# Two steps of a top-k attention kernel change engines: places behind the scores filled on GpSimd, two of nine penalties on VectorE

## The chip, the cores and the metric

The kernel runs on one core of a Trainium2 chip. A core has five engines with queues of their own: TensorE (PE in the profile; its weight loads are PEld), VectorE (DVE), ScalarE (ACT), GpSimd (POOL) and SyncE (SP, which here issues most transfers). Each works its queue in order, and they meet at semaphores. The metric is the device time of one execution in microseconds, taken as the median of several runs.

## The reference, cut to what matters

Attention over 8 batches and 8 heads (sequence 576, head size 64), where each query keeps only its 32 best keys, followed by a mixture of 8 experts over the 4608 tokens:

```python
scores = scale * np.matmul(q, k.transpose(0, 1, 3, 2))
kth = np.partition(scores, -top_k, axis=-1)[..., -top_k:-top_k + 1]
mask = scores >= kth                       # top_k = 32
scores = np.where(mask, scores, -1000000000.0)
...                                        # softmax over the kept ones
return np.matmul(attn, v).astype(np.float32)
# then, per token: skip by the sign of x @ w_skip, choose the expert by argmax of x @ w_gate,
# y = gate * relu(x @ w1[e]) @ w2[e], out = x + y
```

## The kernel before, in words

The 64 heads are worked as 32 pairs. For a pair, the scores of 2 x 576 queries are made in 9 row tiles (`NR = 9`) of 128 queries by `S = 576` keys. Each row tile s goes through a chain that finds its 32nd largest score:

- `qk` (line 666, TensorE): the products, into one of three PSUM buffers r.
- `chunk` (675, VectorE): the 8 largest of each of 7 pieces of the row, seven MAX8 into cand; `cand` (681, 683): five steps, MAX8 and MATCH_REPLACE in turn, that take the 24 largest out of these 56 into cl.
- `take` (694, ScalarE): the scores copied from PSUM to xc. `above_out` (689, ScalarE): r = sign of the 24th candidate less the score, with the sum over the row in CN, which tells how many scores lie above.
- `push_out` (697, GpSimd): xw = xc times r, so that scores above the 24th turn negative. `fill` (706, VectorE): the places behind the 576 scores in xw get large numbers or zero, as many large ones as CN says, so that the next step always finds the 32nd score at place 8. `window` (713, VectorE): the 8 largest of xw, into wn; wn's last is the 32nd score.
- `below_out` (710, ScalarE): PEN = relu(32nd - score), 0 for the keys that are kept.

Two pairs later at most, `block` (804, TensorE) makes the scores again with keys on the partitions, and adds PEN times nbi = -BIG on the identity, so that dropped keys vanish in the exponential (825, ScalarE, into PT). `values` multiplies by v and sums on TensorE in a mode of 32 columns; `prep` makes the next pairs' queries and keys, split into HI (576) and LO = TT - HI (579) on GpSimd; `add` (851, GpSimd) sums two PT tiles; `maxes` (767) and `flags` (717 to 719) are small copies on GpSimd. In the stretch from some 470 to 630 us GpSimd and VectorE also work on `route`, the choice of experts for the first half of the batches.

The order of all this is not written by hand. Every step is a `Task` with an engine, a duration, a due time and the tasks that it waits for; `Plan.run` picks, engine by engine, the task that can start first, and among these the one due first. Due times are the row's number plus an entry of the table `K` plus one of `FINE` for the row's place i in its pair. The result is a fixed program. `DRAIN` is what the plan charges for a change of TensorE's mode.

The lines that the change is about, before:

```python
nc.vector.tensor_scalar(xw()[:, S:S + NF].rearrange("p (a c) -> p a c", a=3), wo[:, :, 0:3], CN[:, s:s + 1], BIG, op0=OP.is_ge, op1=OP.mult)
...
nc.scalar.activation(pen, XC[s], AF.Relu, bias=least, scale=-1.0)
```

After the attention, from about 838 us on, the experts' products fill TensorE (lines 1138 to 1163); `checks` looks at CN and FL there, for rows on which the short way to the 32nd score does not hold.

Of the kernel before, what the change touches and what calls it, by code (L numbers as in the profile page):

```python
# [32 lines left out]
K = dict(qk=-8.256, cand=-59.344, kt=-7.645, push=-28.261, count=0.262, window=9.704, kth=1.605, rf=117.784, pen=-29.958, u0=9.017, u1=9.316, av=-2.884, a0=2.011, a1=2.549, a2=-15.308, co=32.529, sm=-64.563, ca=53.074, tx=-30.308, rt=20.468, rd=-1.415, rs=1.694, pp=14.93, ps=4.136, mx=35.641, f3=20.33, f4=9.022, f5=-15.635, ex=-32.099, us=-0.03, cs=-26.207, ch=-11.218, ce=-46.256, lg=-25.29, ld=12.434, hl=-17.564, hs=-33.172, moe=-7.644)  # L33

FINE = dict(qk=(-10.57, -22.223, -7.096, -21.366, 2.278, -119.12, -31.346, -10.762, 4.455), ch=(12.505, 76.162, -10.027, -38.815, -20.633, 31.276, 34.186, -28.766, -4.283), cand=(6.613, -24.489, -6.913, -22.336, 35.534, -77.941, -24.764, 58.647, -21.15), tx=(-96.011, 71.695, -8.092, -28.201, -15.853, -10.927, -86.098, -6.646, -69.204), kt=(-9.574, -35.926, 21.492, -20.724, -58.083, 108.198, 75.445, 16.722, -3.221), push=(-37.539, 9.983, 6.119, 6.494, -84.073, 20.264, 2.344, 2.351, 10.939), fill=(-25.14, 8.838, 43.271, 3.475, -104.037, -36.948, 24.579, -38.407, 8.32), window=(11.533, -43.047, -0.139, 16.434, -11.305, -22.448, 36.514, 47.528, 5.356), rf=(-13.011, 128.284, 95.339, -40.779, -41.656, -3.528, -16.581, -1.309, -7.056), u=(-2.26, -2.822, -2.506, -3.277, 1.006, -2.132, 3.038, -0.939, -1.738), ex=(-29.429, 18.435, -78.347, -71.269, 37.149, -83.914, -14.847, -34.82, -52.676), f1=(1.311, -59.185, -32.839, -20.531, 4.006, 77.409, -35.268, 14.784, -2.373, -92.948, 24.393, -155.546, -98.645, -15.536, -44.446), f2=(-1.024, -53.705, 3.596, -4.574, -2.423, -3.931, -69.348, -59.52, -5.109), f3=(12.258, -23.157, 17.272, -15.562, 18.297, 1.275), f4=(-10.133, 2.408, -52.184), f5=(0.895, -4.039, -13.889, -126.479, -18.842, -21.09, 31.156, 23.265, -33.592), pp=(5.828, 32.569, 33.595), pa=(-22.396, 0.136, 19.457), hl=(-35.088, -24.202, -29.517, 32.477), mx=(-2.834, 4.967, -17.41, -30.151, -39.559, -52.101), sm=(6.246, -8.842, 17.735, -15.926, -5.444, 7.721))


@with_exitstack
def tile_kernel(ctx, tc, q, k, v, w_skip, w_gate, w1, w2, out):
# [140 lines left out]
    class Plan:  # L180
# [65 lines left out]
        def run(self):  # L246
            picks, dirty = {}, set(ENGS)
            while self.n:
                for e in dirty:
# [24 lines left out]
                for h in x.give:
                    h.give(x)
                    dirty.add("PE")
                for y in x.users + x.next:
                    y.left -= 1
                    y.ready = max(y.ready, x.done + wait(e, y.eng) if y in x.users else t + x.dur)
                    if not y.left:  # L280
                        self.todo[y.eng].append(y)
# [365 lines left out]
    def row(s):  # L647
# [37 lines left out]
        def above_out():  # L685


            RR[s] = wk.tile([P, S], BF, name="r", bufs=3)
            nc.scalar.activation(RR[s], XC[s], AF.Sign, bias=CL[p][:, i, 23:24], scale=-ODD, accum_out=CN[:, s:s + 1])  # L689
# [9 lines left out]
        def xw():  # L699
            if s not in XW:  # L700
                XW[s] = wk.tile([P, S + NF], F32, name="xw", bufs=2)
            return XW[s]

        def fill():

            nc.vector.tensor_scalar(xw()[:, S:S + NF].rearrange("p (a c) -> p a c", a=3), wo[:, :, 0:3], CN[:, s:s + 1], BIG, op0=OP.is_ge, op1=OP.mult)

        def below_out():
            pen, least = PEN[p][:, PS * i + REM:PS * (i + 1)], WN[p][:, i, 7:8]
            nc.scalar.activation(pen, XC[s], AF.Relu, bias=least, scale=-1.0)  # L710

# [547 lines left out]
    def checks():  # L1259
# [7 lines left out]
        for u in range(NR):  # L1267
# [17 lines left out]
        nc.vector.scalar_tensor_tensor(okr, lasf, 1.0, okr, op0=OP.not_equal, op1=OP.mult)  # L1285
        nc.vector.tensor_scalar(okr, okr, 2.0 ** -30, None, op0=OP.is_ge)
        yield
# [267 lines left out]
```

## Time and profile before

| | us |
|---|---|
| median of 3 runs | 1139.01 (1138.16 to 1139.36) |
| profiled execution | 1137.82 |
| its span in the profile | 1135.8 |

Granted TensorE clock over the span: 0.988 of full speed. Busy shares of the whole span, and busy tenths in 40 equal slices of 28.4 us:

```profile
PE 1088.7 (96%) x13000; PEld 934.5 (82%) x13000; DVE 974.7 (86%) x5226; ACT 920.3 (81%) x1902; POOL 752.9 (66%) x949
DVE  8999999999999999999999999999965656655541
ACT  5899999999999999999999999999783533444430
POOL 7678788887787888888998788888784121222211
```

The first 29 or 30 slices are the attention part, the rest the experts. Busy time of PE is modelled at the ends of matmuls, so a busy PE is not PE at its peak. In rows of groups, "busy, mean ns of one" is followed by the idle time just before and what ended it; in rows of waits stand the total, the number and the longest.

### The profile page before, as it was taken

Reading aid. Unit: us, or ns where it says so; the run is one execution under the profiler, and the core shown is the slowest. Engines: PE = TensorE matmul, PEld = TensorE weight load, DVE = VectorE, ACT = ScalarE, POOL = GpSimd, SP = SyncE. Lnnn points to the kernel's source line nnn. Section 1 sums busy time; section 2 is a strip of 40 time slices with the busy share of each in tenths; the row PEclk is TensorE's granted clock in tenths of the full one; section 3 lists DMA queues with packets and bytes.
Section 4 is the critical chain, followed back from the end, with each engine's and each line's share of the span. In section 5 each row is a group of like instructions: output and inputs, shape, how many; then the busy total and the mean of one; then the engine's idle time right before and its main releaser. Section 6 shows DMA issues by size and latency. Waiting matters only on the chain. (4 is left out here: it accounts for less than half of the span.)

```text
span 1135.8 us, 37472 instructions
## 1 busy us (share of the span) xinstructions
PE 1088.7 (96%) x13000; PEld 934.5 (82%) x13000; DVE 974.7 (86%) x5226; ACT 920.3 (81%) x1902; POOL 752.9 (66%) x949
## 2 busy tenths in 40 slices
PE   7999999999999999999999999999899999999996
PEld 5788888888888888888788888888678888999995
DVE  8999999999999999999999999999965656655541
ACT  5899999999999999999999999999783533444430
POOL 7678788887787888888998788888784121222211
PEclk8899999999999999999999999999999999999998
DMA  7645555656555566665545555665147654554300
GB/s 166 126 96 120 125 127 130 148 131 142 117 132 123 125 137 136 148 134 120 127 106 128 127 125 130 138 153 114 44 123 240 187 191 161 169 170 164 121 20 27
DMA packets 239256, 149.06 MB, mean 131 GB/s; under 512 B 141657, under 2 KB 204633, under 8 KB 239057
## 3 DMA queue, kind: packets, MB, share of 16 engines
q1 hardware_dynamic: 232192, 136.19, 49.8%
q0 software_dynamic: 3840, 9.47, 2.4%
q8 instruction: 105, 1.72, 0.6%
q10 hardware_dynamic: 3024, 0.90, 0.3%
q14 instruction: 95, 0.77, 0.2%
HBM read 76.57 MB, written 25.31 MB: 90 GB/s over the span
## 5 line engine op out<-in xcount | busy, mean ns | idle before, releaser
L697 POOL TENSOR_TENSOR xw<-xc,r 128x576 f32<-128x576 f32 x288 | 370.1, 1286 | 117.6 <-ACT r L689 115.4
L675 DVE MAX8 cand<-r 128x8 f32<-128x82 f32 (+1 forms) x2016 | 368.8, 233 | 1.0 <-ACT PEN L710 0.7
L689 ACT ACTIVATE r<-xc,cl 128x576 bf16<-128x576 f32 x288 | 226.4, 786 | 11.7 <-DVE cl L681 8.2
L710 ACT ACTIVATE PEN<-xc,wn 128x576 bf16<-128x576 f32 x288 | 223.3, 787 | 3.6 <-DVE wn L713 3.3
L713 DVE MAX8 wn<-xw 128x8 f32<-128x585 f32 x288 | 217.2, 755 | 2.2 <-POOL xw L697 2.0
L804 PE MATMUL r<-QH,KK 128*128 128x256 f32 (+1 forms) x640 | 187.4, 320 | 6.8 <-ACT PT L825 5.5
L694 ACT ACTIVATE xc<-r 128x576 f32<-128x576 f32 x288 | 186.5, 657 | 6.2 <-DVE cl L681 2.2
L804 PE MATMUL r<-QL,KK 66*128 66x256 f32 (+1 forms) x640 | 172.9, 298 | 0.0
L825 ACT ACTIVATE PT<-r 128x576 f32<-128x576 f32 x256 | 167.7, 656 | 3.1 <-PE r L804 3.1
L681 DVE MAX8 cl<-cand 128x8 f32<-128x28 f32 (+2 forms) x864 | 165.7, 193 | 4.1
L666 PE MATMUL r<-KK,QH 128*128 128x288 f32 x640 | 158.3, 337 | 6.5 <-DVE KK L622 2.4
L1067 POOL DMA_INDIRECT out_dram<-ot,idx x24 | 24.4, 1016 | 190.4 <-DVE ot L1066 146.9
L804 PE MATMUL r<-nbi,PEN 128*128 128x128 bf16 (+1 forms) x1632 | 125.9, 215 | 15.1 <-ACT PT L825 11.1
L666 PE MATMUL r<-KK,QL 65*128 65x288 f32 x640 | 134.0, 300 | 0.0
L804 PEld LDWEIGHTS r<-QH,KK 128*128 128x128 f32 x640 | 117.8, 190 | 15.9 <-ACT PT L825 11.2
L1030 ACT ACTIVATE hi<-raw 128x1024 fp32r<-128x1024 f32 x64 | 67.0, 1056 | 78.7 <-PE py L1163 70.7
L1033 DVE TENSOR_TENSOR lo<-raw,hi 128x1024 fp32r<-128x1024 f32 x60 | 73.2, 1224 | 62.1 <-ACT hi L1030 62.1
L666 PEld LDWEIGHTS r<-KK,QH 128*128 128x128 f32 x640 | 98.2, 193 | 26.5 <-issue 12.8
L804 PEld LDWEIGHTS r<-QL,KK 66*128 66x128 f32 x640 | 118.7, 191 | 0.0
L804 PEld LDWEIGHTS <-PEN 128*128 128x128 bf16 x1632 | 87.3, 98 | 33.5 <-issue 14.2
L666 PEld LDWEIGHTS r<-KK,QL 65*128 65x128 f32 x640 | 103.1, 193 | 0.2 <-DVE QL L622 0.2
L683 DVE MATCH_REPLACE8 cand<-cl,cand 128x28 f32<-128x28 f32 (+1 forms) x576 | 103.0, 179 | 0.0
(272 smaller groups left out, 2453.2 us busy)
## 6 DMA issues: line engine op xcount, KB each, us to landing
raw<-in_moe_w_dram SPq DMA_DIRECT2D x64, 512.0 KB, 4.0
KK<-HI SPq DMA_DIRECT2D x62, 288.0 KB, 3.5
QH<-HI SPq DMA_DIRECT2D x124, 144.0 KB, 3.5
KK<-LO SPq DMA_DIRECT2D x62, 144.0 KB, 3.2
QL<-LO SPq DMA_DIRECT2D x62, 144.0 KB, 3.3
raw<-in_k_dram SPq DMA_DIRECT2D x64, 128.0 KB, 3.0
V<-in_v_dram SPq DMA_DIRECT2D x32, 256.0 KB, 3.3
out_dram<-xd SPq DMA_DIRECT2D x28, 288.0 KB, 3.3
```

The lines of the kernel that those rows point to most:

```text
L666: nc.tensor.matmul(R(u, w), t[0:k0, c:c + P], KH[i2][0:k0, HB * hd + u:HB * hd + w], start=(k0 == P and x == 0), stop=(k0 < P and x == len ...
L675: nc.vector.max(C[s][:, c], R(CH[c], CH[c + 1]))
L681: nc.vector.max(L[:, 4 * r:4 * r + 8], c)
L683: nc.vector.match_replace(c, L[:, 4 * r - 4:4 * r + 4], c, LOWEST)
L689: nc.scalar.activation(RR[s], XC[s], AF.Sign, bias=CL[p][:, i, 23:24], scale=-ODD, accum_out=CN[:, s:s + 1])
L694: nc.scalar.activation(XC[s], R(), AF.Copy)
L697: nc.gpsimd.tensor_tensor(xw()[:, 0:S], XC[s], RR[s], op=OP.mult)
L710: nc.scalar.activation(pen, XC[s], AF.Relu, bias=least, scale=-1.0)
L713: nc.vector.max(WN[p][:, i], XW[s])
L804: nc.tensor.matmul(*ops, start=half not in [x[0] for x in todo[:j]], stop=half not in rest, skip_group_check=turned)
L825: return pl.add("ACT", 0.535, due + K["ex"] + FINE["ex"][at], lambda: nc.scalar.activation(dst, st["r"], AF.Exp, scale=scale), x, give=[h])
L1033: eng.tensor_tensor(WLO[w][i], WRAW[w][i], WHI[w][i], op=OP.subtract)
```

## The change

1. `fill` moves from VectorE to GpSimd: a subtraction of two tiles, wo - CN, into 7 places instead of 9. For this the scores in xc are scaled by SMALL = 2^-30 (in the same copy), so that any positive whole number is larger than every score and any negative one smaller.
2. For row tiles i = 3 and 7 of each pair, `below_out` moves from ScalarE to VectorE, as a comparison with one tensor as source: 1 where the score is below the 32nd, else 0. BIG becomes 2^120, which restores the weight of the scaled differences of the other seven.
3. The planner's costs: changes of TensorE's mode (INTO, DRAIN), a gap ahead of some products (GAP), rows 0.535 and units 0.785 for each; the two moved steps with their new durations; two added conditions (a pair's transposes behind the HI cast of the pair before, row products of i > 2 behind the units of two pairs before); all of K and FINE are new numbers.

```diff
-BIG = 2.0 ** 90
+BIG = 2.0 ** 120
+SMALL = 2.0 ** -30
+BELOW = (3, 7)
...
-DRAIN, TURN = 0.2, 43.29
+DRAIN, INTO, GAP, TURN = 0.02, 0.13, 0.083, 43.29
...
-    NF = 9
+    NF = 7
...
-    wo = cp.tile([P, 3, 4], F32, name="wo")
-    nc.gpsimd.iota(wo, pattern=[[-6, 3], [-2, 4]], base=S - 2 * (TOPK - 7), ...)
-    nc.gpsimd.memset(wo[:, 2, 1:4], -2.0 * S)
+    wo = cp.tile([P, NF], F32, name="wo")
+    nc.gpsimd.iota(wo, pattern=[[-2, NF]], base=S - 2 * (TOPK - 7) + 1, ...)
...
                     if x.mode != self.mode:
-                        t += DRAIN
+                        t += INTO if x.mode == 32 else DRAIN
                         self.mode = x.mode
+                    if x.kind and not self.round:
+                        t += GAP
...
-            nc.scalar.activation(RR[s], XC[s], AF.Sign, bias=CL[p][:, i, 23:24], scale=-ODD, accum_out=CN[:, s:s + 1])
+            nc.scalar.activation(RR[s], XC[s], AF.Sign, bias=CL[p][:, i, 23:24], scale=-ODD / SMALL, accum_out=CN[:, s:s + 1])
...
-            nc.scalar.activation(XC[s], R(), AF.Copy)
+            nc.scalar.activation(XC[s], R(), AF.Copy, scale=SMALL)
...
-            nc.vector.tensor_scalar(xw()[:, S:S + NF].rearrange("p (a c) -> p a c", a=3), wo[:, :, 0:3], CN[:, s:s + 1], BIG, op0=OP.is_ge, op1=OP.mult)
+            nc.gpsimd.tensor_tensor(xw()[:, S:S + NF], wo, CN[:, s:s + 1].to_broadcast([P, NF]), op=OP.subtract)
...
-            nc.scalar.activation(pen, XC[s], AF.Relu, bias=least, scale=-1.0)
+            if i in BELOW:
+                nc.vector.tensor_scalar(pen, XC[s], least, None, op0=OP.is_lt)
+            else:
+                nc.scalar.activation(pen, XC[s], AF.Relu, bias=least, scale=-1.0)
...
-        fx = A("DVE", 0.129, s + D_["push"] + J("fill"), fill, rr, OUTW[-2:-1])
+        fx = A("POOL", 0.2, s + D_["push"] + J("fill"), fill, rr, OUTW[-2:-1])
...
-        kx = PENNED[s] = A("ACT", 0.672, s + D_["rf"] + J("rf"), below_out, wx, TU.get(p - 2))
+        kx = PENNED[s] = A(*(("DVE", 0.42) if i in BELOW else ("ACT", 0.672)), s + D_["rf"] + J("rf"), below_out, wx, TU.get(p - 2))
```

What this makes of the order is seen in pair 8, one of the even pairs, whose order repeats in the pairs before and after. Names in the rows: out<-in, with buffer numbers; lines of the changed kernel lie 4 to 7 further down (chunk 679, cand 685 and 687, window 720, the penalty on VectorE 715, push 701, fill 710, LO 583, HI 580, sum 858).

VectorE around row 3 of the pair and its window, before (the fill of row 3 is `xw_4648`, its window five chunks later):

```order
L683 MATCH_REPLACE cand_4615<-cl_4342,cand_4615 128x7x4
L706 TENSOR_SCALAR xw_4648<-wo_123,CN_126 128x9
L681 MAX cl_4342<-cand_4615 128x8
L675 MAX cand_4663<-r2_156 128x8
L683 MATCH_REPLACE cand_4615<-cl_4342,cand_4615 128x7x6
L675 MAX cand_4663<-r2_156 128x8
L681 MAX cl_4342<-cand_4615 128x8
L675 MAX cand_4663<-r2_156 128x8 x5
L713 MAX wn_4343<-xw_4648 128x8
```

The fill is gone from there. VectorE now, from row 3's penalty (`PEN0_201<-xc_4614`) to row 4's window (`xw_4714`):

```order
L679 MAX cand_4709<-r2_155 128x8
L687 MATCH_REPLACE cand_4665<-cl_4359,cand_4665 128x7x6
L679 MAX cand_4709<-r2_155 128x8
L685 MAX cl_4359<-cand_4665 128x8
L679 MAX cand_4709<-r2_155 128x8 x3
L715 TENSOR_SCALAR PEN0_201<-xc_4614,wn_4360 128x576
L685 MAX cl_4359<-cand_4709 128x8
L720 MAX wn_4360<-xw_4714 128x8
```

The penalty stands between a row's last chunk and its first candidate step, two places ahead of the next window. Further on in the pair, VectorE at row 7, its window (`xw_4912`) and its penalty (`xc_4832`):

```order
L685 MAX cl_4899<-cand_4898 128x8
L720 MAX wn_4360<-xw_4912 128x8
L679 MAX cand_4928<-r0_153 128x8 x2
L715 TENSOR_SCALAR PEN0_201<-xc_4832,wn_4360 128x576
L685 MAX cl_4899<-cand_4928 128x8
L679 MAX cand_4998<-r2_155 128x8
```

Here the penalty follows its own row's window at two chunks' distance. GpSimd at the end of the pair before, from row 7's push (`xw_4877`) to the next pair's first row (`xw_5014`):

```order
L697 TENSOR_TENSOR xw_4877<-xc_4800,r_4852 128x576
L943 TENSOR_TENSOR lg_158<-lg_158,lgt_4875 128x2x2x9
L576 CAST HI_129<-TT_128 128x640 x2
L697 TENSOR_TENSOR xw_4942<-xc_4872,r_4903 128x576
L579 TENSOR_TENSOR LO_130<-TT_128,HI_129 128x640
L697 TENSOR_TENSOR xw_5014<-xc_4967,r_4995 128x576
```

And now, from the sum ahead of it to the next pair's first row (`xw_5012`):

```order
L858 TENSOR_TENSOR sum_4847<-PT0_130 128x576
L950 TENSOR_TENSOR lg_157<-lg_157,lgt_4835 128x2x2x9
L580 CAST HI_128<-TT_127 128x640 x2
L774 CAST NM0_207<-cl_4359 128x4
L710 TENSOR_TENSOR xw_4912<-wo_123,CN_125 128x7
L701 TENSOR_TENSOR xw_4912<-xc_4832,r_4876 128x576
L583 TENSOR_TENSOR LO_129<-TT_127,HI_128 128x640
L710 TENSOR_TENSOR xw_4979<-wo_123,CN_125 128x7
L701 TENSOR_TENSOR xw_4979<-xc_4885,r_4926 128x576
L710 TENSOR_TENSOR xw_5012<-wo_123,CN_125 128x7
```

Each fill now stands ahead of its push, and a LO subtraction directly behind row 7's push, where the two HI casts stood between that push and the next one.

More of the change, by code (lines that the diff above doesn't have):

```diff
@@ new lines @@
+DRAIN, INTO, GAP, TURN = 0.02, 0.13, 0.083, 43.29
+K = dict(qk=-8.543, cand=-15.083, kt=0.641, push=-15.471, count=0.262, window=-4.445, kth=1.605, rf=24.177, pen=-29.958, u0=7.338, u1=11.714, av=-8.454, a0=-11.233, a1=-5.352, a2=13.3, co=39.882, sm=-23.106, ca=53.074, tx=12.855, rt=7.719, rd=13.521, rs=0.505, pp=-1.174, ps=14.228, mx=-2.994, f3=12.416, f4=52.975, f5=21.746, ex=-16.886, us=-3.268, cs=-21.736, ch=-3.905, ce=-12.018, lg=15.965, ld=12.313, hl=4.176, hs=-7.114, moe=7.778)
+FINE = dict(qk=(-12.87, -13.071, -0.344, -26.066, 4.762, -15.372, -7.663, -0.205, 5.146), ch=(3.582, 14.88, -6.257, -19.664, 1.084, 4.045, 6.598, -14.85, 8.09), cand=(-6.274, 0.043, -19.338, 9.135, 3.386, 4.725, -6.454, -13.932, -19.095), tx=(-2.799, 16.941, 5.973, -1.758, -14.865, 25.1, -5.775, -4.793, -16.542), kt=(5.187, -8.053, -11.18, 9.905, 13.525, -13.317, -12.528, 9.006, 4.973), push=(11.95, 8.137, 4.28, 2.957, -7.633, -17.997, 6.536, 14.0, -1.622), fill=(-2.25, -25.583, -7.589, -4.801, -9.466, 2.719, 0.196, 13.815, -9.43), window=(7.295, -3.217, 17.228, 8.542, -15.004, -7.732, 21.554, 14.087, -0.102), rf=(-19.604, 13.641, -0.544, -17.392, -7.293, 11.12, -8.241, 9.439, -2.146), u=(5.016, 3.153, 6.815, 9.245, 0.177, 3.228, 8.968, 10.542, -3.11), ex=(-4.089, -9.336, -14.813, 8.475, -12.628, 3.76, -7.448, 20.175, 2.359), f1=(17.187, -2.992, 1.004, 5.716, -0.479, 52.969, -11.568, 21.046, -4.222, 6.826, -4.425, -13.086, -13.917, 1.599, -2.937), f2=(19.781, -9.808, 3.596, 18.59, -8.525, -3.931, -8.164, -16.856, -5.109), f3=(14.766, 11.443, -3.211, -11.216, -13.714, -15.862), f4=(7.784, 9.035, -35.608), f5=(-8.395, -16.083, -14.55, 15.552, -3.473, 13.474, -8.661, 14.986, 19.967), pp=(-11.882, 9.279, -25.414), pa=(-16.671, -6.231, 19.662), hl=(-4.523, -0.717, 3.198, 15.585), mx=(-28.121, 4.967, -17.41, -14.055, -39.559, -52.101), sm=(10.394, -8.842, 17.735, -13.775, -5.444, 7.721))
@@ L567, in prep @@
             due = NR * p - K["pp"] + K["ps"] * j
-            x = pl.add("PE", 0.11 * len(g), due + FINE["pp"][j], turn(h, g), [LOADED[nm, p] for nm in nms], take=h)
+            x = pl.add("PE", 0.11 * len(g), due + FINE["pp"][j], turn(h, g), [LOADED[nm, p] for nm in nms],
+                       [HIGH[nm, p - 1] for nm in nms if p > 1], take=h)
             y = pl.add("ACT", 0.478 if len(g) > 1 else 0.265, due + 0.1 + FINE["pa"][j], lambda h=h, nms=nms: put(h, nms), x,
@@ L590, in prep @@
             due = NR * p - K["hl"] + K["hs"] * nm
-            x = pl.add("POOL", 0.73, due + FINE["hl"][2 * nm], lambda nm=nm: high(nm), puts[nm], CFREE.get(nm))
+            x = HIGH[nm, p] = pl.add("POOL", 0.73, due + FINE["hl"][2 * nm], lambda nm=nm: high(nm), puts[nm], CFREE.get(nm))
             y = SPLIT[nm, p] = pl.add("POOL", 1.53, due + FINE["hl"][2 * nm + 1], lambda nm=nm: low(nm), x)
@@ L602, in prep @@
             COPIED[p] += c
-    CFREE = {}
+    CFREE, HIGH = {}, {}
     def first(puts):
@@ L722, in row @@
         J = lambda nm: FINE[nm][i]
-        x = ROWQ[s] = A("PE", 0.54 * len(st), s + D_["qk"] + J("qk"), qk, ready(p, i >= NM), CHUNK.get(s - 1), take=h, lag=0.09, kind="row")
+        x = ROWQ[s] = A("PE", 0.535 * len(st), s + D_["qk"] + J("qk"), qk, ready(p, i >= NM), CHUNK.get(s - 1), TU.get(p - 2) if i > 2 else None, take=h, lag=0.09, kind="row")
         chs = []
@@ L822, in f @@
             st["r"] = block(p, whats, h.t, pl.turned)
-        x = pl.add("PE", 0.86 if len(whats) == 1 else 1.65, due + FINE["u"][at], f, after, war, MAXED[p, 0], ready(p, whats[-1][0]), None if p else KOCOPIED, take=h, kind="unit")
+        x = pl.add("PE", 0.785 * len(whats), due + FINE["u"][at], f, after, war, MAXED[p, 0], ready(p, whats[-1][0]), None if p else KOCOPIED, take=h, kind="unit")
         TU[p].append(x)
@@ L1273, in checks @@
             yield
-        nc.vector.scalar_tensor_tensor(okr, FL[:, 0], 2.0 ** 30, FL[:, 1], op0=OP.mult, op1=OP.add)
+        nc.vector.scalar_tensor_tensor(okr, FL[:, 0], 2.0 ** 30 * SMALL, FL[:, 1], op0=OP.mult, op1=OP.add)
         nc.vector.scalar_tensor_tensor(okr, okr, 0.0, FL[:, 3], op0=OP.is_ge, op1=OP.mult)
@@ L1285, in checks @@
         nc.vector.scalar_tensor_tensor(okr, lasf, 1.0, okr, op0=OP.not_equal, op1=OP.mult)
-        nc.vector.tensor_scalar(okr, okr, 2.0 ** -30, None, op0=OP.is_ge)
+        nc.vector.tensor_scalar(okr, okr, 2.0 ** -30 * SMALL, None, op0=OP.is_ge)
         yield
```

4 lines of the change are left out of this document (1 added, 3 removed).

## The prediction

> **What bounds the kernel now.** I read the busy time by stage first, then the waits inside the longest even stage, then single instructions there. The stages: the attention part does 32 pairs of heads with 9 row tiles each; 119.68 to 447.64 us is its even middle, 472.46 to 631.27 us the part where routing work is mixed in, 631.27 to 782.30 us even again.
>
> ```profile
> core 0: us, PE busy (x) PEld busy (x) DVE busy (x) ACT busy (x) POOL busy (x), PEclk, DMA share, GB/s
> 119.68:447.64 327.96, 321.38 (x4603) 275.30 (x4604) 324.37 (x1990) 326.21 (x703) 262.06 (x313) 1.00 0.58 132
> 472.46:631.27 158.81, 152.69 (x2182) 128.99 (x2171) 155.96 (x940) 153.75 (x327) 139.62 (x185) 1.00 0.58 126
> 631.27:782.30 151.03, 147.99 (x2120) 126.98 (x2124) 149.43 (x917) 150.22 (x325) 121.26 (x149) 1.00 0.59 132
> ```
>
> The same stretches counted for the push on GpSimd alone (line 697, one for each row tile):
>
> ```profile
> 119.68:447.64 327.96, 150.62 (x117) 1.00 0.58 132
> 472.46:631.27 158.81, 69.42 (x54) 1.00 0.58 126
> ```
>
> 117 rows are 13 pairs, so a pair takes 327.96 / 13 = 25.23 us; 54 rows are 6 pairs of 26.47 us. VectorE and ScalarE are busy for 99% of the even stretch, and asked for their waits there the profile lists none for either. The other two wait:
>
> ```profile
> PE r L804 <- ACT PT L825: 6.6, 26, 0.3
> POOL xw L697 <- ACT r L689: 51.2, 65, 2.0
> ```
>
> So two engines are the bound together: taking work from one alone gains nothing. TensorE has 327.96 - 321.38 = 6.58 us without work, 0.51 us a pair, and becomes the bound once both give that up. GpSimd has 65.9 us, 5.07 us a pair, 51.2 of it waiting for the signs r.
>
> **What each part costs, for a pair of 25.23 us.** An instruction's price is the time from its start to the next one's, since neighbours overlap. ScalarE first, then VectorE:
>
> ```profile
> 409.14 0.78 ACT L710 ACTIVATE PEN<-xc,wn 128x576 bf16<-128x576 f32 x1
> 409.81 0.78 ACT L689 ACTIVATE r<-xc,cl 128x576 bf16<-128x576 f32 x1
> ```
> ```profile
> 408.82 0.21 DVE L706 TENSOR_SCALAR xw<-wo,CN 128x9 f32<-128x9 f32 x1
> 408.94 0.09 DVE L683 MATCH_VALUE_LOAD cand<-cl,cand 128x8 f32 x1
> ...
> 409.12 0.24 DVE L675 MAX8 cand<-r 128x8 f32<-128x82 f32 x1
> 409.28 0.20 DVE L681 MAX8 cl<-cand 128x8 f32<-128x56 f32 x1
> 409.40 0.68 DVE L675 MAX8 cand<-r 128x8 f32<-128x82 f32 x4
> 410.11 0.19 DVE L681 MAX8 cl<-cand 128x8 f32<-128x28 f32 x1
> 410.22 0.75 DVE L713 MAX8 wn<-xw 128x8 f32<-128x585 f32 x1
> 410.89 0.07 DVE L683 MATCH_VALUE_LOAD cand<-cl,cand 128x8 f32 x1
> ```
>
> *ScalarE.* Two of nine penalties leave: 2 x 0.67 (409.14 to 409.81) = 1.34 us. It stands at 23.9 us and is no longer the bound. The factor on the copy to xc adds no instruction, and the setup loses one memset: 0.
>
> *VectorE, the fills leave.* 9 x 0.12 (408.82 to 408.94) = 1.08 us.
>
> *VectorE, the two penalties come.* No such instruction is in the trace before. The nearest have one tensor source:
>
> ```profile
> L706 DVE TENSOR_SCALAR xw<-wo,CN x288: 193/211/228, 19.1 to 838.9; 128x9 f32<-128x9 f32 x144
> L499 DVE TENSOR_SCALAR rlo<-i,rank x3: 280/280/281, 874.2 to 874.6; 128x128 bf16<-128x128 f32 x3
> L1286 DVE TENSOR_SCALAR okr<-okr x1: 311/311/311, 978.0 to 978.0; 128x288 f32<-128x288 f32 x1
> ```
>
> Line 499 has the form of the new one: a scalar for each partition, f32 in, bf16 out. From 9 to 128 columns the form grows by 280 - 211 = 69 ns, 0.58 ns a column, which makes 211 + 567 x 0.58 = 540 ns of 576 columns. The fill lasts 211 ns and holds the engine for 120, so the penalty holds it for 540 - 91 = 0.45 us. The upper end is the window's MAX8, one column at a time, 0.67 us (410.22 to 410.89); the lower is line 1286 twice, for twice its columns, less one start (the fill's 211 ns) and the overlap: 2 x 311 - 211 - 91 = 0.32 us. I take 0.45, from the row with the same form: + 0.90 us.
>
> *VectorE, the new order.* A step that reads the one just in front of it starts late: the first candidate step after its own row's last chunk starts 0.26 us after that chunk (four chunks from 409.40, 0.15 apart, so 409.85 to 410.11), behind a chunk of another row 0.16 us (409.12 to 409.28). The order has three such places a pair before and one after: - 2 x 0.10 = - 0.20 us. The window loses 2 of 585 columns, 9 x 2 x 750 / 585 ns (the 0.75 us of 410.22) = - 0.02 us. Together: 25.23 - 1.08 + 0.90 - 0.20 - 0.02 = 24.83 us, if nothing new waits.
>
> *The new wait.* [...]
>
> ```profile
> L461 DVE CAST rri<-rmx x3: 172/681/866, 505.1 to 871.2; 128x20 int32<-128x20 f32 x1, 128x15 int32<-128x15 f32 x1, 128x5 int32<-128x5 f32 x1
> L462 DVE TENSOR_SCALAR rri<-rri x3: 158/161/1044, 510.1 to 871.6; 128x20 int32<-128x20 int32 x1, 128x15 int32<-128x15 int32 x1, 128x5 int32<-128x5 int32 x1
> L473 DVE TENSOR_SCALAR base<-base x1: 2216/2216/2216, 802.7 to 802.7; 128x8 f32<-128x8 f32 x1
> ```
> ```profile
> 791.21 0.68 DVE L461 CAST rri<-rmx 128x15 int32<-128x15 f32 x1
> 792.10 1.04 DVE L462 TENSOR_SCALAR rri<-rri 128x15 int32<-128x15 int32 x1
> ```
> ```profile
> 790.42 1.44 POOL L851 TENSOR_TENSOR sum<-PT 128x576 f32<-128x576 f32 x1
> 791.81 1.30 POOL L697 TENSOR_TENSOR xw<-xc,r 128x576 f32<-128x576 f32 x1
> ```
>
> The cast of 0.17 us ends at 791.89, 0.03 us behind the sum (790.42 + 1.44 = 791.86); the next one, 0.16 us alone, ends at 793.14, 0.03 behind the push (793.11). [...] A penalty that comes while a push runs can therefore wait 0 to 1.3 us, and the whole VectorE queue behind it (candidates, windows, and through them ScalarE's penalties and TensorE's units).
>
> [...]
>
> Which of 0 to 1.3 us it is, the order decides. Row 3's penalty stands two places ahead of row 4's window, which needs the end of row 4's push anyway, so what it waits behind that push is mostly the window's own wait: I take 0. Row 7's stands a window and two chunks, 0.67 + 2 x 0.15 = 0.97 us, behind its own push's end at the earliest; GpSimd goes from that push to the LO subtraction, the first of these rows:
>
> ```profile
> L579 POOL TENSOR_TENSOR LO<-TT,HI 128x640 fp32r<-128x640 f32 x62 | 96.8, 1563 | 0.5
> L697 POOL TENSOR_TENSOR xw<-xc,r 128x576 f32<-128x576 f32 x288 | 370.1, 1286 | 117.6 <-ACT r L689 115.4 <-DVE cand L675 0.4 <-DVE wn L713 0.2
> L943 POOL TENSOR_TENSOR lg<-lg,lgt 64x9 f32<-64x9 f32 x62 | 12.5, 201 | 0.5
> ```
>
> At most 1.56 - 0.97 = 0.59 us of LO are left then, and none if the window came 0.6 us after the push; past that the next push can be in the way. I take 0.2, nearer to none. VectorE then stands at 24.83 + 0.2 = 25.03 us. Both ends stay for the range: 0, and 1.3 us each.
>
> *GpSimd, the fills come.* One between 64x9 and the 128x5 cast lasts about 0.2 us (the row of line 943, 201 ns): 9 x 0.2 = 1.8 us of the 5.07 us that are free, and two penalties can keep it out for 0.45 us each: 2.7 us, 22.9 of 25. On the path each fill stands ahead of its push (row 5's behind), so the window of a row may come 0.2 us later; the lower end is 0, since the 51.2 us of waiting over 117 rows (0.44 a row) show that GpSimd is ahead, the upper 1.8 us a pair if every window waited for its push. No window does now, and the order keeps a row or more between: 0.
>
> *TensorE* loses nothing but gets the two added conditions on the plan (the raw tiles' transposes behind the HI cast, row products behind older units). They move instructions and add none; the order keeps them. If they cost, its 0.51 us of idle time is the cover and is then gone.
>
> *The sum.* 25.23 - 25.03 = 0.20 us a pair over the 13 + 6 even pairs and some 3 of the first 119.68 us: 22 x 0.20 = 4.4 us. The routing stretch: GpSimd is busy 139.62 of 158.81 us; 54 fills add 10.8 and 12 penalties up to 5.4, 155.8 us, so nothing is left to gain there, and 0 to 4 us to lose if its work bunches; I take 0. Everything behind 838 us is unchanged and only starts sooner. The profiled execution took 1137.82 us, 2.0 more than its span of 1135.8; the median of the runs is 1139.01, 1.2 above it. So 1133.4 us for a profiled run, and 1139.0 - 4.4 = 1134.6 us for the median: 1135.
>
> **Rivals.**
>
> *The lock eats more than was freed (slower).* The place is the same two penalties, the price is GpSimd's remaining instruction. Met at random, GpSimd busy 22.9 of 25 us and its instructions 1.3 to 1.6 us long, a penalty waits about 0.9 x 0.65 = 0.6 us, and the rows of lines 461, 462 and 473 show 0.7, 0.9 and 2.0. From 0.4 us a pair on, 24.83 + 0.4, VectorE is back at 25.23. At 0.35 each, 25.53 us, it is 22 x 0.3 = 6.6 us slower, and the routing stretch, where GpSimd is full, adds 2: 1148 us. At 0.6 each, 1159. For it: the order of the two engines is fixed and repeats every pair, so an unlucky place is met every time. Against: GpSimd hangs on VectorE through the signs, so it is not random, and part of a wait is the next window's own. Chance 0.32. [...]
>
> *Nothing moves.* [...] Chance 0.18.
>
> *TensorE becomes the bound.* Both penalties come between two GpSimd instructions or behind one that ends, the waits vanish, and the pair falls until TensorE is full, 24.72 us by its recorded idle time: 22 x 0.51 = 11.2 us, with 1 to 3 us more at the start and in the routing part: 1126. For it: ScalarE's 1.34 us of room let the signs come earlier and keep GpSimd ahead. Chance 0.2, within faster.
>
> **How the numbers follow.** My forecast, a small gain of 3 to 8 us, has 0.30, TensorE's bound 0.20: faster by over 0.2% (2.3 us, about what a measurement of this kernel can tell from none) 0.50, within it 0.18, slower 0.32. The range leaves out 2 in 10: the lower end is TensorE's bound with 3 us more from routing, 1123; the upper the first rival between its two prices, 1151. The forecast's own range is 1131 to 1137.
>
> **What the profile after would show.** Right: line 715 on VectorE at about 0.54 us, ScalarE with 7 penalties a pair and idle 3 to 5% of the even part, VectorE still at 99% without waits, GpSimd near 88%, pairs of about 25.0 us. The lock: line 715 far over 0.54 us, its end just behind a GpSimd instruction's end. [...] TensorE the bound: its idle time gone and waits of VectorE for its row products. Wrong altogether: windows that wait for pushes, the fills' 0.2 us on the path after all; or route work stretched well past 158.81 us.

## The result, and the profile after

The changed kernel takes 1154.87 us (median of 6 runs, 1145.38 to 1160.09); the kernel before took 1139.18 in the runs beside it. The ratio is 1.013, 95% interval 1.0104 to 1.0156: slower by 15.7 us, where a gain of 4 was forecast. The profiled execution took 1154.68 us with a span of 1152.8, 17.0 more than the span before.

The penalty on VectorE, all 64 of them (shortest, median and longest, in ns):

```profile
L715 DVE TENSOR_SCALAR PEN<-xc,wn x64: 497/952/3904, 35.3 to 857.1; 128x576 bf16<-128x576 f32 x64
```

Two populations make this row. Row 3's penalty takes 497 to 510 ns in all pairs from 1 to 16; row 7's takes about 1430 in most of them. Pair 8, whose order the prediction spoke of, on VectorE and then on GpSimd (start, duration):

```profile
250.11 0.75 DVE L720 MAX8 wn<-xw 128x8 f32<-128x583 f32 x1
250.78 0.38 DVE L679 MAX8 cand<-r 128x8 f32<-128x82 f32 x2
251.07 1.43 DVE L715 TENSOR_SCALAR PEN<-xc,wn 128x576 bf16<-128x576 f32 x1
252.42 0.18 DVE L685 MAX8 cl<-cand 128x8 f32<-128x28 f32 x1
```
```profile
249.19 1.56 POOL L583 TENSOR_TENSOR LO<-TT,HI 128x640 fp32r<-128x640 f32 x1
250.71 0.19 POOL L710 TENSOR_TENSOR xw<-wo,CN 128x7 f32<-128x7 f32 x1
250.87 1.28 POOL L701 TENSOR_TENSOR xw<-xc,r 128x576 f32<-128x576 f32 x1
252.12 0.45 POOL L710 TENSOR_TENSOR xw<-wo,CN 128x7 f32<-128x7 f32 x1
```

The penalty comes 0.20 us after row 8's push has started, and ends 0.35 us after the push does, as if the push had to end first: 1.43 - 0.50 = 0.93 us of wait. The small fill behind, 0.20 us elsewhere, takes 0.45 and ends 0.07 us behind the penalty, as if now the penalty were ahead of it. This is what the prediction calls the lock: a VectorE instruction that ends behind one of GpSimd's as if it had to wait for it, as the steps of lines 461 and 462 did in the kernel before (0.03 us behind). But it is not behind the LO subtraction: it is behind the push.

By stage. The rows are the stretch of pairs 2 to 16, of pairs 17 to 24 (with routing work), and, inside the first, of pair 11 alone:

```profile
core 0: us, PE busy (x) PEld busy (x) DVE busy (x) ACT busy (x) POOL busy (x), PEclk, DMA share, GB/s
72.00:459.00 387.00, 377.16 (x5322) 316.78 (x5316) 380.73 (x2191) 362.00 (x781) 325.59 (x496) 0.99 0.56 129
459.00:674.30 215.30, 207.91 (x2901) 172.24 (x2893) 209.69 (x1188) 195.11 (x419) 195.99 (x308) 0.99 0.55 124
302.60:333.00 30.40, 27.13 (x353) 22.97 (x353) 27.80 (x147) 24.31 (x53) 21.07 (x34) 0.89 0.48 109
```

An undisturbed pair takes 25.4 us (25.2 before). Pair 11 takes 30.4, and its granted clock is 0.89. What happened at its start, where row 7 of the pair before is still in work, on GpSimd, VectorE and TensorE:

```profile
301.69 1.28 POOL L701 TENSOR_TENSOR xw<-xc,r 128x576 f32<-128x576 f32 x1
302.93 0.20 POOL L710 TENSOR_TENSOR xw<-wo,CN 128x7 f32<-128x7 f32 x1
303.09 1.27 POOL L701 TENSOR_TENSOR xw<-xc,r 128x576 f32<-128x576 f32 x1
304.33 1.53 POOL L583 TENSOR_TENSOR LO<-TT,HI 128x640 fp32r<-128x640 f32 x1
```
```profile
302.27 3.90 DVE L715 TENSOR_SCALAR PEN<-xc,wn 128x576 bf16<-128x576 f32 x1
```
```profile
306.97 0.85 PE L670 MATMUL r<-KK,QH 128*128 128x288 f32 x2 [3.27 <-ACT xc L698]
```

Here the penalty, issued 0.58 us into a push, does not get in when the push ends: the fill goes first, then another push, then LO. It ends 0.31 us behind LO, 3.90 us after it began. Everything queued behind it on VectorE is late, TensorE stands idle for 3.27 us, and its products then take 0.85 us, where the same line took 0.53 at 301.65: for 6.8 us the clock records grant half speed.

Where the time went, from the starts of the sign instruction (line 689 before, 693 after) in the two traces, with two versions from below beside them (the slow form is that of the first experiment, in which the penalty reads three runs and takes 0.79 us):

| us | before | after | row 7 in the slow form | and row 3 outside the even stages |
|---|---|---|---|---|
| to pair 2 | 68.4 | 72.0 | 72.5 | 72.5 |
| pairs 2 to 16 | 379.3 | 387.0 | 372.9 | 372.8 |
| pairs 17 to 24, routing | 208.8 | 215.3 | 211.3 | 209.5 |
| pairs 25 to 28 | 100.9 | 100.7 | 99.0 | 98.9 |
| pairs 29 to 31 | 80.6 | 80.8 | 81.3 | 81.1 |
| rest | 297.8 | 297.1 | 298.2 | 297.0 |
| span | 1135.8 | 1152.8 | 1135.1 | 1131.9 |

Of the 17.0 us, the even stage has 7.7 (5.2 of it pair 11), the routing stage 6.5, the start 3.6.

### The profile page after: what moved, and what is told of

Same layout as the page of the kernel before. It is cut to its first block, busy times and chain, and to the rows that moved or that the text cites. A ratio compares the mean times of both kernels' runs of the same rounds, so it can differ in the third digit from the quotient of the medians.

```text
span 1152.8 us, 37624 instructions
## 1 busy us (share of the span) xinstructions
PE 1102.5 (96%) x12995; PEld 934.2 (81%) x12995; DVE 985.7 (85%) x5002; ACT 889.3 (77%) x1838; POOL 806.6 (70%) x1236
## 4 chain that ended last, share of the span: by engine, by line
PE 65%; DVE 19%; ACT 5%; issue 4%; SPq 2%; POOL 2%; DMA 1%; ACTq 0%; POOLq 0%; DVEq 0%
PE r L811 14%; PE r L670 11%; PE pa L879 7%; DVE cand L679 7%; PE py L1168 4%; PE py L1170 4%; PE py L1169 4%; PE ph L1145 3%; PE ph L1146 3%; PE ph L1147 3%; DVE wn L720 3%; DVE cl L685 3%; DVE cand L687 2%; PE pa L896 2%; PE pa L882 2%
## 5 line engine op out<-in xcount | busy, mean ns | idle before, releaser
L679 DVE MAX8 cand<-r 128x8 f32<-128x82 f32 (+1 forms) x2016 | 391.3, 233 | 11.2 <-PE r L670 7.2
L720 DVE MAX8 wn<-xw 128x8 f32<-128x583 f32 x288 | 215.8, 750 | 3.3 <-POOL xw L701 3.3
L698 ACT ACTIVATE xc<-r 128x576 f32<-128x576 f32 x288 | 188.9, 657 | 32.0 <-DVE cl L685 24.0
L811 PE MATMUL r<-QH,KK 128*128 128x320 f32 (+1 forms) x640 | 184.1, 315 | 1.2 <-ACT xc L698 0.5
L717 ACT ACTIVATE PEN<-xc,wn 128x576 bf16<-128x576 f32 x224 | 176.2, 789 | 2.8 <-DVE wn L720 2.5
L811 PE MATMUL r<-QL,KK 66*128 66x320 f32 (+1 forms) x640 | 174.0, 299 | 0.0
L832 ACT ACTIVATE PT<-r 128x576 f32<-128x576 f32 x256 | 164.1, 652 | 7.9 <-PE r L811 7.5
L685 DVE MAX8 cl<-cand 128x8 f32<-128x28 f32 (+2 forms) x864 | 162.2, 188 | 2.3
L879 PE MATMUL pa<-PT,V 128*32 128x256 f32 (+1 forms) x2464 | 122.5, 330 | 0.7 <-ACT os L905 0.4
L710 POOL TENSOR_TENSOR xw<-wo,CN 128x7 f32<-128x7 f32 x288 | 64.7, 225 | 73.6 <-ACT r L693 68.4
```

The costliest lines, as they stand in the source:

```text
L679: nc.vector.max(C[s][:, c], R(CH[c], CH[c + 1]))
L685: nc.vector.max(L[:, 4 * r:4 * r + 8], c)
L698: nc.scalar.activation(XC[s], R(), AF.Copy, scale=SMALL)
L720: nc.vector.max(WN[p][:, i], XW[s])
L811: nc.tensor.matmul(*ops, start=half not in [x[0] for x in todo[:j]], stop=half not in rest, skip_group_check=turned)
L832: return pl.add("ACT", 0.535, due + K["ex"] + FINE["ex"][at], lambda: nc.scalar.activation(dst, st["r"], AF.Exp, scale=scale), x, give=[h])
```

## The experiments

In the diffs, "..." stands for lines left out.

**Take the lock away, and nothing else.** The xc tile gets two gaps, so that the penalty reads three runs of 192 columns; the old fill, which was never held up (228 ns at most, 211 in the middle, in the 288 of the kernel before), read 3x3 in the same manner.

```diff
-            XC[s] = wk.tile([P, S], F32, name="xc", bufs=3)
+            XC[s] = wk.tile([P, 3, S // 3 + 1], F32, name="xc", bufs=3)[:, :, 0:S // 3]
...
-            pen, least = PEN[p][:, PS * i + REM:PS * (i + 1)], WN[p][:, i, 7:8]
+            pen, least = PEN[p][:, PS * i + REM:PS * (i + 1)].rearrange("p (a c) -> p a c", a=3), WN[p][:, i, 7:8]
```

The copy, the sign and the push are written as 3 x 192 in the same way.

> The changed kernel, same order of instructions; the copy xc lies in three runs of 192 columns with one unused column behind each, so that the two penalties on VectorE read 3x192 and not one run of 576, as the old fill read 3x3. Lock theory (the two penalties run in the fast form, which GpSimd's instructions hold up): the penalty goes one column a cycle, about 0.75 us each in every row and stage, without waits; VectorE has 25.4 - 0.92 + 2 x 0.26 = 25.0 us a pair, the pairs of 30 us and the drops of TensorE's clock in the middle go, and the kernel takes 1134 to 1143 us. Rival (GpSimd's nine fills a pair, or the new order itself, cost the time): the waits were not what mattered, VectorE gets 0.5 us a pair more, and the kernel takes 1155 to 1167 us.

Measured: 1139.74 us, 0.9993 of the kernel before (0.9977 to 1.0008). Its penalties:

```profile
L715 DVE TENSOR_SCALAR PEN<-xc,wn x64: 782/794/812, 35.1 to 844.2; 128x576 bf16<-128x576 f32 x64
```

Each is 0.29 us slower by itself, none waits in any stage, pairs take 25.1 us, and the kernel is 15 us faster than the changed one. Fills and order are the same in both, so the waits are the loss, and neither the fills nor the order. The source is now three runs with gaps and the destination three runs that touch, and the penalty takes 794 ns in the middle where one run of 576 took some 500. That this form would not be held up was the author's estimate from the old fill, and the run bears it out; why three runs take longer is not shown. No run shows what a cycle is: the "column a cycle" of the expectations stands for these 794 ns for 576 columns, and the window's "one column at a time" of the prediction for 749 ns for 583 (line 720).

**Row 7 alone in that form.** As above, for i = 7 only:

```diff
+        part = lambda t: t.rearrange("p (a c) -> p a c", a=3) if i == 7 else t
...
+            xc = wk.tile([P, S + 3], F32, name="xc", bufs=3)
+            XC[s] = xc.rearrange("p (a c) -> p a c", a=3)[:, :, 0:S // 3] if i == 7 else xc[:, 0:S]
...
```

> The changed kernel with the three-run copy for row 7 alone: its penalty goes a column a cycle (0.79 us) and cannot be held up, that of row 3 keeps the fast form (0.50 us), which waited for nothing in the even part. Lock theory: VectorE has 25.4 - 0.92 + 0.26 = 24.75 us a pair, so TensorE bounds at 24.9; the pair takes 24.9 to 25.0 us, and the kernel 1134 to 1140 us, 0 to 5 us less than with both penalties in that form. If row 3's penalty was not harmless (pile-ups, the routing stage) it takes 1143 us or more.

Measured: 1136.64 us, 0.9977 (0.9963 to 0.9991), a little faster than before. Pairs 2 to 16, and a row 7 with the push beside it:

```profile
72.50:445.40 372.90, 372.39 (x5322) 314.16 (x5314) 369.01 (x2191) 361.99 (x781) 321.29 (x496) 1.00 0.59 133
```
```profile
247.17 0.79 DVE L718 TENSOR_SCALAR PEN<-xc,wn 128x576 bf16<-128x576 f32 x1
```
```profile
246.89 1.29 POOL L704 TENSOR_TENSOR xw<-xc,r 128x576 f32<-128x576 f32 x1
```

The penalty comes 0.28 us into the push, the same unlucky place, and takes its 0.79 us all the same. Pairs take 24.8 us and TensorE is busy for 372.39 of 372.90: the third rival's bound, reached with row 7 repaired and row 3 left as it was.

**And row 3 too, outside the even stages.** Against the version just shown:

```diff
-        part = lambda t: t.rearrange("p (a c) -> p a c", a=3) if i == 7 else t
+        split = i == 7 or not 2 <= p < 17 and not 25 <= p < 29
+        part = lambda t: t.rearrange("p (a c) -> p a c", a=3) if split else t
...
```

> The changed kernel with the three-run copy for row 7 in all pairs, and for row 3 outside the even stages (pairs 0, 1, 17 to 24 and 29 to 31) too; only row 3's penalty in the even pairs keeps the fast form. With the copy for row 7 alone, row 3's penalties of those 13 pairs waited 0.4, 0.4, 1.1, 0.1, 2.0, 0.4 and 0.1 us for GpSimd, 4.5 us in all, and 13 x 0.29 = 3.8 us are paid for the slower form. Lock theory: nothing is held up any more; 0 to 4 us less than with row 7 alone (more than the 0.7 us of the sum if the long waits cost TensorE its clock), so 1132 to 1137 us. Rival (the routing stage is long because of the order and not of the lock): no change, its eight pairs stay at 211 to 213 us.

Measured: 1134.32 us, 0.9959 (0.9945 to 0.9972): the fastest of all these. No penalty takes over 0.82 us now, and the routing pairs fall from 211.3 to 209.5 us; before they took 208.8. That is 5.8 of the 6.5 us that the routing stage lost, but not all of it is shown to be the penalties' share: in the first experiment all penalties there have the slow form too, and the stage still took 213.3 us, 2.0 less than in the changed kernel. In both, a routing step on VectorE with two tensor sources, 0.26 us where nothing holds it, was held up behind three GpSimd instructions. The changed kernel, then the first experiment, then this one:

```profile
615.79 3.43 DVE L493 TENSOR_TENSOR rrh<-i,rcol 128x120 bf16<-128x120 f32 x1
```
```profile
602.78 3.38 DVE L493 TENSOR_TENSOR rrh<-i,rcol 128x120 bf16<-128x120 f32 x1
```
```profile
599.89 1.83 DVE L493 TENSOR_TENSOR rrh<-i,rcol 128x120 bf16<-128x120 f32 x1
```

In the first two TensorE then idled 1.8 us, and its clock fell to half. GpSimd's order there is the same in all three (push, HI, LO); here the step got in ahead of LO.

**Move row 7's penalty earlier.** Same order, but issued directly behind its window instead of two chunks later:

```diff
         def window():
             nc.vector.max(WN[p][:, i], XW[s])
+            if i == 7:
+                below_out(True)
...
```

> The changed kernel with one step moved: the penalty of row 7 is issued right behind its window, two chunk maxima (0.3 us) earlier, before the push of row 8 starts; nothing else changes place. Lock theory: it holds VectorE 0.5 us or little more and the push of row 8 starts some 0.2 to 0.4 us later; the 0.92 us a pair are gone, the pair falls from 25.4 to 24.5 to 25.0 us (TensorE was busy 24.9 of 25.1 in the one-port kernel, so it bounds), and the kernel takes 1130 to 1142 us. Rival (the wait only moves: it meets the LO subtraction or the fill instead, or the later push makes a window wait): 25.2 to 25.5 us a pair and 1146 to 1156 us.

Measured: 1163.22 us, 1.021 (1.0192 to 1.0227). My expectation was wrong. VectorE and then GpSimd in pair 7:

```profile
225.11 1.62 DVE L717 TENSOR_SCALAR PEN<-xc,wn 128x576 bf16<-128x576 f32 x1
```
```profile
225.06 1.27 POOL L701 TENSOR_TENSOR xw<-xc,r 128x576 f32<-128x576 f32 x1
```

GpSimd moved too: the push now starts 0.05 us ahead of the penalty, which waits for all of it, 1.1 us a pair (pairs of 25.9 us). The penalty of pair 13 took 4.41 us, and pair 14 took 30.8.

**Move it later.** Issued behind the fourth candidate step of row 1 of the next pair, six steps on, wherever row 8's window has not been issued yet:

```diff
+            if i == 7 and not late and not PAST & {(s + 3, "cand"), (s + 1, "window")}:
+                LATE[s] = lambda: below_out(True)
+                return
...
```

> The changed kernel with one step moved the other way: row 7's penalty, still in the fast form, is issued six candidate steps later (behind the fourth candidate step of the row after next but one, where the order still allows it), some 0.9 us behind its old place, so near the end of the push of row 8 and not at its start. Lock theory (a penalty that comes while a push runs waits for the rest of that push): the wait falls from 0.92 us to 0 to 0.4 us a pair, VectorE has 24.5 to 24.9 us, TensorE bounds at 24.8; pairs of 24.8 to 25.0 us and 1133 to 1143 us. Rival (VectorE loses what GpSimd holds wherever the penalty stands, since GpSimd is busy 21.7 of 25.4 us): 0.6 to 1.3 us of wait again, pairs of 25.2 to 25.9 us and 1148 us or more.

Measured: 1256.21 us, 1.104 (1.1016 to 1.1064). Wrong again, and by far. The stretch of pairs 2 to 16, and the penalty of pair 6 on VectorE, then GpSimd and TensorE:

```profile
68.90:523.20 454.30, 407.73 (x5322) 345.50 (x5318) 402.03 (x2191) 364.88 (x780) 322.37 (x496) 0.90 0.48 110
```
```profile
218.31 2.77 DVE L725 TENSOR_SCALAR PEN<-xc,wn 128x576 bf16<-128x576 f32 x1
```
```profile
218.01 1.26 POOL L708 TENSOR_TENSOR xw<-xc,r 128x576 f32<-128x576 f32 x1
219.24 1.52 POOL L583 TENSOR_TENSOR LO<-TT,HI 128x640 fp32r<-128x640 f32 x1
```
```profile
221.88 0.85 PE L670 MATMUL r<-KK,QH 128*128 128x288 f32 x2 [3.32 <-ACT xc L705]
```

The penalty now meets the push behind row 8's, 0.30 us after its start, and loses to the LO subtraction as well. What the changed kernel shows once, at pair 11, is here in nearly every even pair: 2.77 us on VectorE, 3.3 us of idle TensorE, half clock, 30.6 us.

**Fills back on VectorE, the new order kept.** Nine places again, as before:

```diff
-            nc.gpsimd.tensor_tensor(xw()[:, S:S + NF], wo, CN[:, s:s + 1].to_broadcast([P, NF]), op=OP.subtract)
+            nc.vector.tensor_scalar(xw()[:, S:S + NF].rearrange("p (a c) -> p a c", a=3), wo[:, :, 0:3], CN[:, s:s + 1], 2.0 ** 90, op0=OP.is_ge, op1=OP.mult)
...
```

> The changed kernel, its own order, with the fills back on VectorE in the old form (nine columns, 3x3 view); the order that was planned for fills on GpSimd is kept. Lock theory: VectorE gets 1.08 us a pair more on top of the 25.4, so 26.3 to 26.5 us a pair and 1175 to 1185 us; the waits of row 7's penalty stay or grow. Rival (GpSimd's load by the fills makes the loss): with GpSimd relieved of 1.8 us a pair the kernel takes no longer than the changed one, 1145 to 1158 us.

Measured: 1156.21 us, 1.0133 (1.0103 to 1.0163), the number of the rival; but its reason is not the rival's. VectorE is full (25.4 of 25.5 us a pair), and the penalties hardly wait:

```profile
L716 DVE TENSOR_SCALAR PEN<-xc,wn x64: 493/548/3306, 36.3 to 859.4; 128x576 bf16<-128x576 f32 x64
```

The nine fills put GpSimd and VectorE elsewhere against each other: row 3's penalty stays free, and row 7's now comes some 1.04 us into a push, close to its end, and waits 0.06. VectorE pays 1.08 us a pair for the fills and is spared 0.93 of wait. My lock theory had kept the wait in place, which is why its 1175 to 1185 us were at least 19 us too high.

**The fills alone, in the old order** (all penalties on ScalarE; the kernel before, with the new scale, seven places and)

```diff
-            nc.vector.tensor_scalar(xw()[:, S:S + NF].rearrange("p (a c) -> p a c", a=3), wo[:, :, 0:3], CN[:, s:s + 1], BIG, op0=OP.is_ge, op1=OP.mult)
+            nc.gpsimd.tensor_tensor(xw()[:, S:S + NF], wo, CN[:, s:s + 1].to_broadcast([P, NF]), op=OP.subtract)
...
```

> The kernel before, in its own order, with only the fills changed: subtraction on GpSimd in seven columns, with the new scale; all nine penalties stay on ScalarE. Lock theory with two bounds: VectorE falls by 1.08 us a pair, ScalarE stays full, so the even pair stays at 25.1 to 25.3 us and the kernel takes 1135 to 1142 us. Rival (the fills on GpSimd are what costs): GpSimd has 1.8 us a pair more, windows come to wait for fills and pushes, and the kernel takes 1146 us or more.

Measured: 1159.68 us, 1.017 (1.0147 to 1.0194). Pairs take 26.0 us with no engine full, and VectorE has waits in the twelve pairs from 121.7 us on that it did not have before:

```profile
DVE wn L713 <- POOL xw L706: 9.3, 12, 0.8
DVE wn L713 <- POOL xw L697: 2.7, 12, 0.2
```

In the old order the fill follows its push, and the window waits for both, 1.0 us a pair. This is the rival of the expectation: fills on GpSimd are not free in any order, and here they cost 20 us.

**The penalties alone, in the old order,** in the fast form, and in the slow form with xc in three runs as above:

```diff
-            nc.scalar.activation(pen, XC[s], AF.Relu, bias=least, scale=-1.0)
+            if i in BELOW:
+                nc.vector.tensor_scalar(pen, XC[s], least, None, op0=OP.is_lt)
+            else:
+                nc.scalar.activation(pen, XC[s], AF.Relu, bias=least, scale=-1.0)
...
```

> The kernel before, in its own order, with only the penalties of rows 3 and 7 moved to VectorE in the form of the changed kernel; the fills stay on VectorE. Lock theory: VectorE has 25.23 + 2 x 0.41 us a pair and whatever the two wait for GpSimd, 0 to 1.3 us each: 26.1 to 27.5 us a pair, and the kernel takes 1160 to 1195 us, with penalties that end just behind a GpSimd instruction. Without a lock it would be 26.05 us a pair and 1157 to 1162 us, all penalties at 0.5 us.

> The kernel before, in its own order, with only the two penalties moved to VectorE as in the run with the penalties alone (1205 us, 27.5 us a pair), but in the form that reads three runs: a column a cycle, about 0.79 us each. Lock theory: VectorE has 25.2 + 2 x 0.70 = 26.6 us a pair, and though each penalty is slower by itself the pair falls by 0.9 us and the kernel takes 1176 to 1188 us. Rival (the order of before can't take the penalties, whatever their form): 27.4 us a pair or more and 1200 us or more.

Measured: 1205.2 us (1.056, 1.0532 to 1.0588), above the 1160 to 1195 expected, and 1181.5 us (1.037, 1.0355 to 1.0385), as expected. Their penalties:

```profile
L712 DVE TENSOR_SCALAR PEN<-xc,wn x64: 498/1132/1806, 30.6 to 908.0; 128x576 bf16<-128x576 f32 x64
```
```profile
L712 DVE TENSOR_SCALAR PEN<-xc,wn x64: 786/796/812, 30.6 to 886.7; 128x576 bf16<-128x576 f32 x64
```

In this order both penalties of a pair meet a push, 0.6 and 0.8 us of wait. The form that is 0.29 us slower is 24 us faster, 26.6 against 27.5 us a pair. So the penalties are held up in the old order and with the old fills too: 1132 ns in the middle, 498 at the least.

**The new order alone** (fills and penalties on their old engines, new offsets), and **the penalties back on ScalarE** (fills on GpSimd). Both have, of the changed kernel,

```diff
-            if i in BELOW:
-                nc.vector.tensor_scalar(pen, XC[s], least, None, op0=OP.is_lt)
-            else:
-                nc.scalar.activation(pen, XC[s], AF.Relu, bias=least, scale=-1.0)
+            nc.scalar.activation(pen, XC[s], AF.Relu, bias=least, scale=-1.0)
```

and the first has the fills back on VectorE as well.

> The changed kernel's order and new scale, but fills and all nine penalties where they were before (fills on VectorE in nine columns, penalties on ScalarE); the plan still counts them on the new engines. It is what the new offsets are worth alone. VectorE would have 24.5 + 1.08 - 0.82 = 24.8 us a pair and ScalarE 24.1 + 1.34 = 25.4: ScalarE bounds, 25.3 to 25.5 us a pair, 1140 to 1150 us. If the new order loses in the stage with routing work by itself, its eight pairs stay near the 213.5 us of the one-port kernel (208.8 before) and not near the 215.2 of the changed one. Rival (the new offsets are a gain of their own and only the lock eats it): 25.0 us a pair and 1137 us or less.

> The changed kernel with both penalties back on ScalarE in the places they have in the new order; fills stay on GpSimd. No instruction of the row work on VectorE can then be held up by GpSimd. Lock theory: VectorE 23.7 us a pair, ScalarE 24.1 + 1.34 = 25.4 and the bound: 25.3 to 25.6 us a pair, no pile-up, 1140 to 1152 us. Rival (fills on GpSimd cost by themselves, as in the kernel before with the fills alone, where neither engine was full in pairs of 26.0 us): 25.8 to 26.2 us a pair and 1155 us or more.

Measured: 1163.23 us (1.021, 1.0195 to 1.0224) and 1158.21 us (1.016, 1.0145 to 1.0174); pairs of 25.9 and 25.6 us, ScalarE busy for 25.3 of them. Both times lie above what was expected, the second in the range of its rival: ScalarE is the fullest engine, but does not get quite full, and the routing pairs take 216.7 and 220.2 us. That the other VectorE steps of the rows are not held up by GpSimd is what the changed kernel's trace shows: its chunks, candidate steps and windows take 254, 222 and 771 ns at most. So the new offsets are no gain by themselves, and penalties on VectorE are worth having once they don't wait: from 1158 to 1137 us with row 7 in the slow form.

**A plan that knows the lock** (a penalty may start only when GpSimd's instruction before has ended, and keeps it out):

```diff
-                r = x.ready
+                r = max(x.ready, self.at["POOL"]) if x.kind == "port" else x.ready
...
```

> The changed kernel and its offsets, with the plan told of the lock: it lets a penalty on VectorE start only when GpSimd's instruction before has ended, and keeps GpSimd out until the penalty is done. The whole order comes out otherwise, in the routing stage too. Lock theory: most penalties then take 0.5 us, few over 0.8; pairs of 24.8 to 25.2 us; 1128 to 1142 us. Rival (the plan's times differ from the chip's by more than the gaps between GpSimd's instructions, so it cannot steer it): waits of 0.5 to 1.3 us remain in half of the penalties or more, and the kernel takes 1146 us or more.

Measured: 1265.3 us, 1.1103 (1.1084 to 1.1122). Neither case: most penalties are short (median 504 ns), 16 of 64 still take over 0.8 us (longest 1723), and it is the slowest of all. The offsets were made for another rule; under this one the pairs no longer repeat (24 to 38 us each) and TensorE idles up to 5.2 us at a time. It tells that a plan can avoid most of the waits, and nothing of what that would bring with offsets of its own.

## Why the prediction was wrong, point by point

- *ScalarE at 23.9 us a pair:* 362.00 / 15 = 24.1. Near enough; it was not the bound.
- *VectorE at 24.83 without waits:* 25.4 - 0.93 = 24.5. The penalty was put at 0.54 us and takes 0.50; the rest of the 0.3 us is not accounted for.
- *Row 3's penalty waits 0:* right in the even stage, 497 to 510 ns. In the routing and end stages and in pair 0, which the prediction did not look at, single ones took 0.8 to 1.6 us.
- *Row 7's penalty waits 0.2:* **the step that failed.** It was argued from the LO subtraction, with a half sentence for the next push, and the push is what it meets: 0.93 us in nearly every even pair. In pair 8 the LO subtraction had ended at 250.75, 0.32 us before the penalty came. The sum then has VectorE at 25.4, above the 25.23 of before, instead of 25.03. The choice "nearer to none" rested on no row, since 0.2 us more or less of either engine decides between 0 and a whole push.
- *The first rival, 1148 at 0.35 us each and 1159 at 0.6:* this is what came. Measured are 0 and 0.93, 0.46 on average, and 1155 us. Its "the order is fixed, so an unlucky place is met every time" is what the even pairs show. Its price was put together otherwise, though: the even pairs lose only 0.17 us each.
- *Nothing moves, chance 0.18:* no run shows a ground for it in the changed kernel, whose penalties take 497 to 3904 ns and whose time moved by 15.7 us. The first experiment came out there (1139.74 us, 0.79 us a penalty without a wait), but with xc in three runs.
- *The upper bound of 1.3 us a wait, and what it left without a term:* a penalty that loses several times in a row. The prediction's own row of line 473 (2216 ns for 128x8) had waited some 2.0 us, behind a push of 1.28 us and the GpSimd work after it; the penalty of pair 10 waited 3.4. One pair of 30.4 us cost 5.2 in the profiled execution. That the changed kernel's runs spread over 14.7 us (1145 to 1160) would fit pile-ups that come in some runs and not in others, and so would their granted clocks, 0.986 in the shortest and 0.976 in the longest; only one of them, of 1154.68 us, has a trace.
- *Routing stage, 0 to 4 us lost, 0 taken:* 6.5. Between 2.0 and 5.8 of it are the penalties' waits, as the two versions without them put it; how often line 493 loses to GpSimd makes the difference uncertain.
- *Three pairs of gain at the start:* the start lost 3.6 us, and lost 4.1 in the two repaired versions, so not to the lock. In the changed kernel's trace TensorE idles 2.6 and 2.8 us there, between 9 and 18 us, and has 27.3 us of half clock in the first 61, 17.1 of them on end; before it had 20.5. With the new order alone the start took 70.7 us, 2.3 more than before, so part of the loss is the order's; how it comes about is not shown.
- *Fills 0.2 us on GpSimd, 0 on the path:* right, 201 ns in the middle, and no window of the changed kernel waits for one in the even pairs. The longest (up to 507) come where a penalty goes ahead of them, as at 252.12. The second half holds for the new order; in the old one the windows waited.

```profile
L710 POOL TENSOR_TENSOR xw<-wo,CN x288: 191/201/507, 20.6 to 856.8; 128x7 f32<-128x7 f32 x144
```

- *TensorE becomes the bound, 1126 us:* 24.8 us a pair (24.72 foretold) in the repaired versions; they gain 6.4 us in the stretch of pairs 2 to 16 and 1.9 in pairs 25 to 28, but nothing at the start nor in routing.

## What to carry to other kernels

Before an instruction like this penalty (one source, 0.50 us when nothing holds it) goes to VectorE, look at what GpSimd runs at the moment it will be issued: here a push of 1.28 us held row 7's up by 0.93 in nearly every even pair, and the form that is 0.29 us slower cost less (1136.64 us with row 7 in it, against 1154.87). Where two engines depend on each other, moving the instruction a few places moves the other engine too: here 0.3 us earlier made 0.93 into 1.1, and six steps later made it 2.3. A change made for another reason, the fills back on VectorE, made it 0.06. The price of a stall is what stands idle behind it, so look for the longest single wait and at the granted clock there (a penalty of 3.90 us, then 0.89 in pair 11), not at the median alone (0.95 us).

## What the runs showed of the hardware that was not expected

*A waiting VectorE instruction was not always next.* Behind the push of 250.87 us the penalty went ahead of the fill; behind that of 301.69 it lost to three more instructions, and with the later penalty it lost to LO in nearly all even pairs, by like distances (0.20, 0.58, 0.30 us into the push). With the penalties alone it came 0.32 us into the push and went ahead of LO in nearly every pair. It is not the penalties alone: line 493, with two tensor sources, lost to a push, a HI cast and LO (3.43 us) and elsewhere to the first two only (1.83). The wait in pair 8 was for one push of 1.28 us, and a LO subtraction takes 1.58 at most in the changed kernel; waits of 3.4 us were seen, and of 3.9 with row 7 earlier. What decides who is next stays open.

*Half clock followed gaps in TensorE's work.* Over the traces of all fourteen kernels, between 60 and 860 us: of 28 idle stretches over 2.4 us, 27 had half clock begin in them or within 4.5 us behind them (18 of the 28 are from one kernel, that with the later penalty); of 14 between 1.8 and 2.4 us, 12; of 27 between 1.4 and 1.55 us, 2. The half clock lasted 3.4, 6.8 or 10.2 us. So in these traces a wait that left TensorE idle for some 2 us or more mostly cost twice: the gap, and half speed behind it.
